# Seven products for eight in the second MoE matmul: Strassen's algorithm on pairs of token tiles, with its sums on VectorE

## The chip, the cores and the metric

One core of one Trainium2 chip runs the kernel. The metric is the device time of one execution in microseconds (us), given as the median of several executions. The profile is taken of one execution, so its span differs a little from the median. PE is TensorE, DVE is VectorE, ACT is ScalarE, POOL is GpSimd, SP is SyncE; a q behind the name (SPq, ACTq) is the engine's sequencer, which here issues DMAs.

## The reference, cut to what matters

```python
# q, k, v: (8 batches, 12 heads, 448 tokens, 64); w_in: 768 x 2048; w_out: 2048 x 768
scores = q @ k.T / sqrt(64)
attn   = softmax(scores) @ v              # (8, 12, 448, 64)
x      = attn, heads side by side          # 3584 tokens x 768
h      = x @ w_in                          # first MoE matmul, 3584 x 2048
g      = h * sigmoid(h)
out    = g @ w_out                         # second MoE matmul, 3584 x 768, fp32
```

## The kernel before

Everything runs in fp16 with fp32 sums in PSUM, and the kernel's buffers there limit how much work may be under way: four banks are shared by h, the attention output a, and the outputs of the second matmul; two tiles of two banks each take scores. A score matmul uses only 32 of the 128 rows of the array (one head's half), and the kernel issues four of them for four different strips of rows, which overlap in the trace. A *burst* is a set of scores between two other kinds of work. Each score tile holds two heads. A burst for one score tile is called "one-bank" here, a burst for both tiles "both-bank".

The second matmul gives one PSUM bank 16 products of 128 tokens by 384 outputs, one for each 128 of the 2048 inner elements; ScalarE copies the bank out and SyncE's queue stores it:

```python
def ffn2(u, t, half):                      # 28 token tiles x 2 halves
    o = ps.tile([128, 512], FP32, tag="m", bufs=4)
    for f in range(NFF):                   # 16
        nc.tensor.matmul(out=o[:, 0:OH],   # OH = 384
            lhsT=g_t[(u, f)][:, 128 * t : 128 * (t + 1)],
            rhs=w_out_t[:, f, n0:n1], start=(f == 0), stop=(f == NFF - 1))

def store(u, t, half):
    ost = sb.tile([128, OH], FP32, tag="ost", bufs=6)
    nc.scalar.copy(out=ost, in_=o_t[(u, t, half)][:, 0:OH])
    for w in range(4):
        ...
        last = (u, t, half) == (B // 2 - 1, NT - 1, 1)
        eng = nc.scalar if last and w % 2 else nc.sync      # two queues at the very end
        eng.dma_start(out=dst[col // 32], in_=ost[32 * w : 32 * (w + 1), :])
```

The order of the instructions is worked out while the kernel is built, by a list scheduler in the kernel's own file: it keeps a clock, an estimated duration for each operation, and a count of free buffers ("rings"), and puts on each engine what is ready first. The parts (`...` marks cuts):

```python
t = sb.tile([128, TPP, 2, 32], FP16, name=f"rk_{b}_{hg}", tag="rk", bufs=3)   # raw k
t = sb.tile([128, g1 - g0, 2, 32], FP16, name=f"rq_{n}", tag="rq", bufs=4)    # raw q
...
rk_ring, rq_ring, v_ring = Ring(3), Ring(4), Ring(2)     # the scheduler's view of them
...
# scores of units 0 to 2 go bank by bank, later ones in both-bank bursts
split = ((0,), (1,)) if ns[0] < 3 else ((0, 1),)
...
for i in range(NWARM):                                   # 13 matmuls of zeros at the start ("warming")
    nc.tensor.matmul(out=z, lhsT=zeros[:, 0:128], rhs=zeros, start=True, stop=True)
```

The softmax here doesn't subtract the row's maximum and nothing guards it: scores larger than these inputs give would overflow.

## Time and profile before

| | before |
|---|---|
| time, median (range) of 3 | 425.92 us (425.27 to 426.13) |
| span of the profiled execution | 423.6 us |
| TensorE busy | 414.5 us, 98% |
| VectorE / ScalarE busy | 193.8 us / 242.5 us |
| first h product / first output product | 25.64 us / 60.18 us after the start |
| last product to end of span | 4.01 us |

The prediction below shows the page's head, the cut by stages and the prices. Two views that it tells but does not show are needed. The first is the waits of TensorE (columns: who waited, for whom; us in total, times, longest):

```profile
PE s L295 <- ACT E L331: 2.9, 6, 1.0
PE h L414 <- DVE g L432: 0.5, 1, 0.5
```

So TensorE waits for the exponentials at the start, and hardly for anything else. The second is the end of the timeline (columns: start us, duration, engine, line, what, how many):

```profile
404.86 16.07 SPq L464 DMA_DIRECT2D out_dram<-ost  x25
...
419.64 0.48 ACT L457 COPY ost<-o 128x384 f32<-128x384 f32 x1 [2.12 <-PE o L445]
420.15 0.86 ACTq L464 DMA_DIRECT2D out_dram<-ost  x2
```

(The view merges rows of one kind: the 16.07 us hold pauses of the queue.) The last copy follows the last product at once, and the last four stores go out on two queues, which are done 1.4 us after the last product (at 419.56).

### The profile page before, as it was taken

How to read it: one execution, taken by the hardware profiler on the slowest of the kernel's cores; microseconds unless marked ns; L12 is line 12 of the kernel's file. 1: busy time of each engine (PE TensorE's matmuls, PEld its weight loads, DVE VectorE, ACT ScalarE, POOL GpSimd, SP SyncE). 2: the span in 40 equal slices, each digit the busy share in tenths (PEclk: the TensorE clock that was granted, in tenths of full speed). 3: DMA queues.
4: the chain of work that ended last, by engine and by line, in shares of the span. 5: the costliest groups of instructions: out<-in, count | busy, mean ns of one | idle time of the engine just before them, and what ended most of it. 6: DMA issues, size and time to landing. Idle time of an engine off the chain costs nothing.

```text
span 423.6 us, 9512 instructions
## 1 busy us (share of the span) xinstructions
PE 414.5 (98%) x3933; PEld 212.4 (50%) x3933; DVE 193.8 (46%) x404; ACT 242.5 (57%) x373; POOL 95.3 (22%) x175
## 2 busy tenths in 40 slices
PE   7899999999999999999999999999999999999996
PEld 3567755444544444444344545544445565565563
DVE  4568746667333585725577154512354204403400
ACT  4678975697465777667766753465773114414411
POOL 6775656630005406200440700000000000000000
PEclk9589999999999999999999999999999999999999
DMA  8999999890024906712390941012100220031033
GB/s 119 201 194 184 148 182 218 126 174 3 15 63 65 204 5 90 125 44 53 34 165 21 156 91 39 2 28 53 34 2 11 51 67 24 2 74 40 0 76 74
DMA packets 37979, 34.45 MB, mean 81 GB/s; under 512 B 11952, under 2 KB 36400, under 8 KB 37936
## 3 DMA queue, kind: packets, MB, share of 16 engines
q0 software_dynamic: 27184, 22.82, 36.7%
q1 hardware_dynamic: 10656, 10.93, 10.1%
q8 instruction: 31, 0.51, 0.5%
q10 hardware_dynamic: 96, 0.10, 0.1%
q14 instruction: 12, 0.10, 0.1%
HBM read 45.61 MB, written 11.01 MB: 134 GB/s over the span
## 4 chain that ended last, share of the span: by engine, by line
PE 93%; ACT 2%; DMA 1%; POOL 1%; DVE 0%; issue 0%; ACTq 0%; DVEq 0%
PE o L445 35%; PE h L414 33%; PE a L347 14%; PE s L295 10%; ACT E L331 2%; PE z L856 1%; DMA rk<-in_k_dram 1%; POOL V L235 1%; DVE KT L271 0%; POOL rq L222 0%; POOL rk L216 0%; DVE g L432 0%; ACT ost L457 0%; DVE zeros L199 0%; DVE ones L197 0%
## 5 line engine op out<-in xcount | busy, mean ns | idle before, releaser
L331 ACT ACTIVATE E<-s 128x896 f16<-128x896 f32 (+1 forms) x172 | 148.9, 914 | 24.2 <-PE s L295 22.9
L414 PE MATMUL h<-xT,w_in_t 128*128 128x448 f16 (+1 forms) x864 | 153.6, 332 | 0.5 <-DVE g L432 0.5
L445 PE MATMUL o<-w_out_t,g 128*128 128x384 f16 x896 | 152.5, 326 | 0.0
L432 DVE SCALAR_TENSOR_TENSOR g<-th,h 128x448 f16<-128x448 f16 (+1 forms) x144 | 79.8, 564 | 98.2 <-ACT th L425 96.3
L445 PEld LDWEIGHTS <-g 128*128 128x128 f16 x896 | 84.7, 98 | 65.1 <-issue 11.6
L414 PEld LDWEIGHTS <-w_in_t 128*128 128x128 f16 x864 | 80.8, 98 | 69.2 <-issue 13.6
L425 ACT ACTIVATE th<-h 128x448 f16<-128x448 f32 (+1 forms) x144 | 71.6, 505 | 53.2 <-PE h L414 52.1
L457 ACT COPY ost<-o 128x384 f32<-128x384 f32 x56 | 26.8, 479 | 99.5 <-PE o L445 92.3
L235 POOL DMA_DIRECT2D V<-in_v_dram x88 | 48.9, 572 | 134.8 <-PE a L347 113.1
L295 PE MATMUL s<-QT,KT 32*128 32x448 f16 (+4 forms) x864 | 54.1, 344 | 3.2 <-ACT E L331 2.9
L271 DVE STREAM_TRANSPOSE KT<-rk 128x256 f16<-128x256 f16 (+2 forms) x96 | 31.7, 380 | 46.0 <-PE s L295 26.4
L400 DVE SCALAR_TENSOR_TENSOR xT<-a,rdn 128x448 f16<-128x448 f32 (+1 forms) x54 | 29.0, 568 | 34.0 <-PE a L347 33.7
L347 PE MATMUL a<-E,V 128*32 128x448 f16 (+3 forms) x864 | 42.0, 346 | 0.2 <-issue 0.2
L295 PEld LDWEIGHTS <-KT 32*128 32x128 f16 (+2 forms) x864 | 16.6, 101 | 32.0 <-issue 30.6
L347 PEld LDWEIGHTS <-V 128*32 128x32 f16 (+2 forms) x864 | 19.0, 98 | 23.5 <-issue 16.3
L282 DVE STREAM_TRANSPOSE QT<-rq 128x896 f16<-128x896 f16 (+1 forms) x27 | 26.3, 976 | 0.9 <-DMA rq<-in_q_dram 0.9
L383 DVE STREAM_TRANSPOSE sT<-a 128x448 f32<-128x448 f32 (+1 forms) x27 | 14.8, 576 | 26.0 <-PE a L347 26.0
L347 PE MATMUL a<-E,ones 128*32 128x448 f16 (+4 forms) x432 | 21.8, 349 | 0.0
L222 POOL DMA_DIRECT2D rq<-in_q_dram x27 | 15.5, 574 | 4.2 <-DMA rk<-in_k_dram 1.2
L347 PEld LDWEIGHTS <-ones 128*32 128x32 f16 (+2 forms) x432 | 9.5, 99 | 12.7 <-issue 9.0
L392 DVE STREAM_TRANSPOSE rdn<-inv 128x448 f32<-128x448 f32 (+1 forms) x27 | 14.5, 563 | 0.1
L216 POOL DMA_DIRECT2D rk<-in_k_dram x24 | 13.9, 580 | 2.8 <-DMA w_out_t<-in_moe_w_out_dram 1.7
(12 smaller groups left out, 33.3 us busy)
## 6 DMA issues: line engine op xcount, KB each, us to landing
out_dram<-ost SPq DMA_DIRECT2D x222, 48.0 KB, 1.6
rk<-in_k_dram POOLq DMA_DIRECT2D x24, 224.0 KB, 5.5
rq<-in_q_dram POOLq DMA_DIRECT2D x21, 224.0 KB, 6.3
w_in_t<-in_moe_w_in_dram POOLq DMA_DIRECT2D x24, 128.0 KB, 5.1
w_out_t<-in_moe_w_out_dram POOLq DMA_DIRECT2D x8, 384.0 KB, 8.7
V<-in_v_dram POOLq DMA_DIRECT2D x43, 64.0 KB, 4.7
V<-in_v_dram POOLq DMA_DIRECT2D x40, 48.0 KB, 4.5
rq<-in_q_dram POOLq DMA_DIRECT2D x6, 112.0 KB, 5.8
```

Source lines behind the costliest of these rows:

```text
L235: nc.gpsimd.dma_start(out=VT[b][32 * x : 32 * (x + 1), hs, 0:count, :], in_=v[b, hs].rearrange("h (i g) d -> i h g d", g=TPP)[:, :, first ...
L271: nc.vector.transpose(out=kt[:, e].rearrange("p c x i -> p x c i")[:, x:y, 0:count], in_=t[:, first : first + count * (y - x), e, :].rearr ...
L282: nc.vector.transpose(out=qt.rearrange("p e g i -> p g e i"), in_=rawq[n])
L295: nc.tensor.matmul(out=pS[p0 : p0 + 32 * (x1 - x0), h % 2, at : at + nq], lhsT=KT[(b, hg)][32 * h : 32 * (h + 1), e, c, x0:x1, :], rhs=QT[ ...
L331: nc.scalar.activation(out=E[(n, w)][0:kr, 2 * y : 2 * y + 2, :], in_=pS_t[(n, w, y)][0:kr, :, 0:S], func=AF.Exp, scale=attn_scale,)
L347: nc.tensor.matmul(out=a[32 * h : 32 * (h + 1), 0:nq], lhsT=w, rhs=e[k0:k1, h, at : at + nq], start=start, stop=stop,)
L400: nc.vector.scalar_tensor_tensor(out=xT[(b, cc)][:, 32 * g0 : 32 * g1], in0=acc[(n, part)][:, 0:nq], scalar=0.5, in1=rdn_t[n].rearrange("p ...
L414: nc.tensor.matmul(out=h[:, 0 : t1 - t0], lhsT=w_in_t[:, cc, 128 * f : 128 * (f + 1)], rhs=xT[(b, cc)][:, t0:t1], start=(cc == 0), stop=(c ...
L425: nc.scalar.activation(out=th, in_=h_t[(b, f, t0)][:, 0 : t1 - t0], func=AF.Tanh)
L432: nc.vector.scalar_tensor_tensor(out=g_t[(u, f)][:, S * r + t0 : S * r + t1], in0=th_t[(b, f, t0)], scalar=1.0, in1=h_t[(b, f, t0)][:, 0 : ...
L445: nc.tensor.matmul(out=o[:, 0:OH], lhsT=g_t[(u, f)][:, 128 * t : 128 * (t + 1)], rhs=w_out_t[:, f, n0:n1], start=(f == 0), stop=(f == NFF ...
L457: nc.scalar.copy(out=ost, in_=o_t[(u, t, half)][:, 0:OH])
```

## The change

Its intent is to make TensorE, which sets the end, do less. Two token tiles A (rows) by two halves of the inner elements, times two halves of the inner elements by two halves of the outputs, is a 2 x 2 matrix product of blocks. Strassen's algorithm does it with 7 block products (8 matmuls each) for 8, and pays with sums of blocks before and after. Thirteen of the fourteen pairs of tiles take it; the first stays plain, as the weight sums are not ready. The core of the diff:

```diff
-    def ffn2(u, t, half): ...            # 16 matmuls into one bank
+    def combine_g(qd, m, f0, f1):        # sums of gate outputs, fp16, VectorE
+        x, y, op = {
+            5: (rows(a, 0), rows(a, 1), ALU.add),
+            2: (rows(b, 0), rows(b, 1), ALU.add),
+            1: (rows(a, 0), rows(b, 1), ALU.add),
+            6: (rows(b, 0), rows(a, 0), ALU.subtract),
+            7: (rows(a, 1), rows(b, 1), ALU.subtract),
+        }[m]
+        ...
+        nc.vector.tensor_tensor(out=dst[:, f0:f1], in0=x[:, f0:f1], in1=y[:, f0:f1], op=op)
+
+    BANK = {3: 3, 5: 3, 4: 4, 2: 4, 1: 1, 7: 1, 6: 6}    # 5, 2, 7 accumulate on 3, 4, 1
+    def product(qd, m): ...              # 8 matmuls, 384 columns each
+    def take_3(qd):   nc.scalar.copy(out=tmp(qd, "s"), in_=bank(qd, 3))
+    def take_4(qd):   add(tmp_t[(qd, "s")], bank(qd, 4), tmp_t[(qd, "s")])
+    ...                                  # six fp32 sums of 384 elements for each pair
+    def take_7(qd):
+        add(ost(qd, 0, 0), bank(qd, 1), tmp_t[(qd, "s")])
+        store(qd, 0, 0)
```

`combine_w` makes the five weight sums once, in the same way, in ten instructions. With the algorithm came a new frame around it: smaller buffers, to make room in SBUF, another pacing of the scores, and other rules for the start:

```diff
-    PACE = 2.6
+    PACE = 3
-        t = sb.tile([...], FP16, name=f"rk_{b}_{hg}", tag="rk", bufs=3)     # ring 3 -> 2 too
+        t = sb.tile([...], FP16, name=f"rk_{b}_{hg}", tag="rk", bufs=2)
-        t = sb.tile([...], FP16, name=f"rq_{n}", tag="rq", bufs=4)          # ring 4 -> 3 too
+        t = sb.tile([...], FP16, name=f"rq_{n}", tag="rq", bufs=3)
-            split = ((0,), (1,)) if ns[0] < 3 else ((0, 1),)
+            split = ((0,), (1,)) if ns[0] < 6 else ((0, 1),)
-    for i in range(NWARM): ...           # 13
+        if warm["on"] and od.free["PE"] <= od.now and wait > 0.3 and od.now > 1.0:
+            n = max(1, int((wait - 0.1) / mm(512)))      # comes to 20
+            od.on_pe(Op("PE", n * mm(512), lambda n=n: run_zeros(n)), "full")
-            eng = nc.scalar if last and w % 2 else nc.sync
+            nc.sync.dma_start(...)       # all stores on one queue
```

## The prediction

> **What bounds the kernel now.** I read first the page's table of busy time, its row of slices and its chain, to see which engine sets the end.
>
> ```profile
> span 423.6 us, 9512 instructions
> ...
> PE 414.5 (98%) x3933; PEld 212.4 (50%) x3933; DVE 193.8 (46%) x404; ACT 242.5 (57%) x373; POOL 95.3 (22%) x175
> ...
> PEclk9589999999999999999999999999999999999999
> ...
> PE 93%; ACT 2%; DMA 1%; POOL 1%; DVE 0%; issue 0%; ACTq 0%; DVEq 0%
> PE o L445 35%; PE h L414 33%; PE a L347 14%; PE s L295 10%; ACT E L331 2%; PE z L856 1%; DMA rk<-in_k_dram 1%; POOL V L235 1%; DVE KT L271 0%; POOL rq L222 0%; POOL rk L216 0%; DVE g L432 0%; ACT ost L457 0%; DVE zeros L199 0%; DVE ones L197 0%
> ```
>
> TensorE is on the chain for 93% of the span, and the largest item on it, 35%, is "o", the second MoE matmul, which is what the change cuts. A busy PE alone proves little, because matmul records overlap; the chain and the absence of waits prove more. The cut by stages then shows where TensorE is really full (columns: stretch; length; PE, PEld, DVE, ACT, POOL busy with counts; granted clock; DMA share; GB/s).
>
> ```profile
> 0.00:10.00 10.00, 7.49 (x45) 3.11 (x46) 4.15 (x13) 3.68 (x4) 7.12 (x16) 1.00 0.81 114
> 10.00:20.00 10.00, 8.59 (x128) 5.41 (x127) 5.99 (x16) 6.99 (x9) 7.45 (x14) 0.52 1.27 200
> 20.00:30.00 10.00, 9.68 (x184) 6.57 (x184) 5.23 (x16) 7.07 (x12) 6.91 (x14) 0.79 1.11 200
> 30.00:40.00 10.00, 9.69 (x200) 7.57 (x192) 7.98 (x23) 8.93 (x16) 6.91 (x12) 1.00 1.13 177
> 40.00:280.00 240.00, 239.51 (x2392) 115.57 (x2390) 131.66 (x272) 160.12 (x241) 66.91 (x122) 1.00 0.56 91
> 280.00:420.00 140.00, 139.56 (x1005) 74.13 (x1003) 38.84 (x67) 55.55 (x95) 0.00 (x0) 1.00 0.16 39
> ```
>
> From 40 us on TensorE stands still for about 1 us of 380, at full clock, with VectorE 55% busy up to 280 us and 28% after. So a TensorE microsecond removed there is worth a microsecond, until another engine cannot follow. The first 40 us are another regime: half clock between 10 and 24 us, ACT and DMA in the way.
>
> Last I took the price of one product, from the groups by form and from the chain in order of time.
>
> ```profile
> L445 PE MATMUL o<-w_out_t,g 128*128 128x384 f16 x896 | 152.5, 326 | 0.0
> L457 ACT COPY ost<-o 128x384 f32<-128x384 f32 x56 | 26.8, 479 | 99.5 <-PE o L445 92.3 <-issue 7.2
> ...
> 63.45 2.71 PE o L445 x16
> 66.67 2.71 PE o L445 x16
> ...
> 398.76 20.81 PE o L445 x128
> ```
>
> The last row is the clean price: 128 back-to-back products in 20.81 us, 0.1626 us each (384 columns). The two rows above show a product group that alternates with a score burst of 8 matmuls: the period is 66.67 - 63.45 = 3.22 us, of which 16 x 0.1626 = 2.60 is product and 0.37 the burst (8 matmuls of 448 columns, four at a time, at 448/384 of the column time: 2 x 0.187). The rest, 0.25, is two changes between the whole array and its row tiles: about 0.11 to 0.12 us each.
>
> [...]here the 13 warming matmuls took 5.73 us, 0.44 us each, twice the full-clock time of 512 columns (0.217 by the same scaling).
>
> **The change part by part.** There are 28 token tiles, 14 pairs. The first pair stays plain: 4 groups of 16. Thirteen pairs take 7 products of 8 matmuls.
>
> Removed from TensorE: 896 - (64 + 13 x 56 = 728) = 104 matmuls. At 0.1626 us: -16.9 us. All lie after 60 us, so on the path.
>
> Added to TensorE: from the built instruction order the array changes mode 222 times instead of 200; 22 x 0.11 = +2.4 us. The order also has 20 warming matmuls for 13, 19 of them before the first scores. In the kernel before, the 13 end at 6.96 us just as the first transposed q is ready (6.94), so they cost nothing; six more at 0.22 to 0.44 us put the first scores back by 1.3 to 2.6 us, less if the clock comes up earlier. I take +1.5.
>
> Recovered at the start: units 3 to 5 now issue their scores one bank at a time, so that ACT can run exp on one while TensorE fills the other. Before, ACT shows gaps of 1.56, 1.57, 0.59 and some 0.3 us there, about 4 in sum; the array is at half clock, so I credit half: -2.
>
> [...]ACT loses 13 of 56 copies, 13 x 0.479 = -6.2 us, and goes to 236. [...]a gate or a reading of PSUM that comes late holds one of the four PSUM banks that h, a and p share. [...]I take +2 for TensorE waits, where there was 1.
>
> Moved: products 5, 2 and 7 accumulate on the bank of 3, 4 and 1 after that was read, so TensorE now depends on a copy or a sum in the middle of a pair. In the built order another pair's product or an attention step nearly always stands between [...], so I count nothing extra. Buffers for k, q, their transposes, E and xT shrink by a tenth to a third, to make room. The loads are asked for at 0.56 of the DMA in the middle stage, so I expect no loss after 60 us.
>
> The end: before, 4.0 us pass from the last product (419.57) to the end. Now product 6's four stores occupy the one SP queue (0.42 us an issue by the trace's median) until about 1.1 us after the last product, [...]its four issues end at 2.8; before, the two queues were done 1.4 us after the last product. So +1.4.
>
> Sum: -16.9 + 2.4 + 1.5 - 2.0 + 2.0 + 1.4 = -11.6; with 425.9 that makes 414.3. The order was evidently tuned anew with it (pacing of scores, priorities, starts allowed before the last operand of a group is there), which on average recovers something, so I set 413.5.
>
> **The rivals.** (1) VectorE becomes the bound in places. For: [...]four shared banks, a fresh dependence of sums on the last gates. Against: [...]the first three or four products of a pair need no sum. If it holds in half of the stretches, 8 to 12 us of TensorE waits come back: 421 to 425, within 2%. (2) The shared banks or smaller buffers give waits of TensorE on ACT or DMA. For: bank 3 of a pair is held across two products and two readings. Against: the interleaving of pairs. It would show as 3 to 6 us: 417 to 419. [...](4) TensorE saved all and nothing is given back: 425.9 - 16.9 = 409; with a better start 406.
>
> **Range and chances.** The arithmetic of products is sure to a microsecond; the start is good for 3 us either way, VectorE for 0 to 10 on the slow side. So 407 to 420 should hold it 8 times in 10. Faster by over 2% means under 417.4: it is about 4 us above my point, with one-sided risk from VectorE, 0.79. Within 2%: 0.18. Slower by over 2% needs the waits to exceed the whole saving by 8 us: 0.03.
>
> **What would show it.** Right: 792 product matmuls with about 134 us busy; idle TensorE time from 40 us on under 4 us; [...]the chain still over 90% TensorE; full clock from 40 us. Wrong: [...]TensorE rows with idle time released by VectorE sums or gates; loads of k, q and v landing later than now; the first scores after 9 us, or half clock beyond 25 us.

Passages that no trace or run of this case supports are cut out of the prediction, and the cuts are marked: all but the last measurement of one paragraph, the price of the added work on VectorE (130 gate sums, 78 fp32 sums, 10 weight sums and 32 gates cut in two) with the totals made from it, one rival, a few clauses and two signs. The forecast's sum came to -11.6 us, and 0.8 us for tuning made 413.5 us.

## More of the kernel before

Runs fall into groups by the mean clock that TensorE was granted (0.970 to 0.972 or 0.979 to 0.980 in nine of ten runs of the changed kernel), which turns out to matter. The series ran on different chips of the same kind, on which the median of the kernel before was 425.3 to 426.0 us; small differences between series have to be read with that in mind.

## The result, and the profile after

The changed kernel took 420.37 us (418.59 to 420.78, 4 runs) against 426.02 us (425.27 to 426.27) of the kernel before in the same rounds: a ratio of 0.9862, interval 0.9831 to 0.9894, so within 2%. Ratios here are the mean time of one kernel's runs over that of the other's of the same rounds, so not quite the ratio of the medians. The predicted 413.5 us was 7 us too low and the range, 407 to 420, did not hold it.

The head of the page after, with the chain of what ended last:

```profile
span 419.0 us, 9580 instructions
PE 404.6 (97%) x3836; PEld 203.8 (49%) x3836; DVE 285.2 (68%) x654; ACT 233.4 (56%) x360; POOL 95.2 (23%) x175
PEclk9659999999999999999999999999999999999998
PE 90%; DVE 4%; DMA 3%; issue 1%; ACT 1%; POOL 1%; DVEq 0%; POOLq 0%
```

TensorE is still the bound: 90% of the chain, and VectorE has 32% of its time free. The durations of VectorE's instructions, added up from the traces, rose by 109.9 us (from 211.4 to 321.3); neighbours overlap in time, so the busy time rose by 91.4 only, to 285.2. But the row of clocks (in tenths, 40 slices) shows 6 and 5 where the kernel before has 5 and 8. The cut by stages says where:

```profile
0.00:10.00 10.00, 7.93 (x44) 3.22 (x45) 3.99 (x12) 3.01 (x4) 6.12 (x15) 1.00 0.70 101
10.00:20.00 10.00, 8.38 (x128) 5.16 (x131) 4.71 (x13) 6.77 (x9) 6.88 (x14) 0.63 1.17 166
20.00:30.00 10.00, 8.91 (x148) 5.65 (x146) 3.85 (x11) 6.19 (x7) 5.88 (x11) 0.50 1.07 185
30.00:40.00 10.00, 10.00 (x152) 6.78 (x144) 6.52 (x20) 7.19 (x12) 8.41 (x14) 0.84 1.10 184
40.00:280.00 240.00, 237.53 (x2331) 116.48 (x2330) 175.96 (x398) 152.33 (x236) 64.63 (x117) 1.00 0.57 92
280.00:420.00 140.00, 131.86 (x1053) 66.56 (x1050) 90.20 (x203) 57.88 (x95) 3.28 (x6) 0.98 0.19 43
```

Asked for as one window, 20 to 40 us holds 292 matmuls on TensorE where the kernel before has 372, and idling explains little of it (1.1 us, before 0.6): the clock is at 0.50 for the whole of the third stretch and back at full speed only at about 33 us (0.84 of the fourth stretch, so 3.2 us of it at half speed), against 24 us before. From 40 us on, TensorE is idle for 2.5 us up to 280 us.

Three marks split the difference of the two profiled spans, 423.6 - 419.0 = 4.6 us. The work before the first output product is nearly the same in both (192 matmuls of h and 336 of attention; 272 of scores for 264, and 20 warming ones for 13), so the mark can be compared:

| stretch | before | after | change | prediction's terms |
|---|---|---|---|---|
| start to first output product | 60.18 | 67.06 | +6.9 | +1.5 - 2.0 = -0.5 |
| first output product to last | 359.38 | 344.79 | -14.6 | -16.9 + 2.4 + 2.0 - 0.8 = -13.3 |
| last product to end | 4.01 | 7.15 | +3.1 | +1.4 |
| sum | 423.6 | 419.0 | -4.6 | -12.4 |

The middle did a little better than predicted. What is missing is 7.4 us at the start and 1.7 us at the end. (Counted in the traces, 9 of the 22 added changes of mode lie before the first output product, so some 1.0 of the +2.4 us belongs to the first row.)

Two details of the new frame show at the start. GpSimd's timeline, first before:

```profile
3.50 0.57 POOL L216 DMA_DIRECT2D rk<-in_k_dram  x1
4.02 0.58 POOL L222 DMA_DIRECT2D rq<-in_q_dram  x1
4.54 2.51 POOL L235 DMA_DIRECT2D V<-in_v_dram  x4
```

and after:

```profile
6.38 0.53 POOL L222 DMA_DIRECT2D rk<-in_k_dram  x1 [2.84 <-DVE KT L277]
6.90 0.55 POOL L228 DMA_DIRECT2D rq<-in_q_dram  x1
7.42 2.49 POOL L241 DMA_DIRECT2D V<-in_v_dram  x4
```

With two k buffers, the third k load has to wait until VectorE has transposed the first k (2.84 us of idle time, released by KT), and V, which GpSimd issues after it, comes 2.9 us later (7.42 for 4.54 us). The other detail is the score bursts. Before, in TensorE's timeline:

```profile
21.88 0.93 PE L295 MATMUL s<-QT,KT 32*128 32x224 f16 x16
```

and after, at the same half clock:

```profile
21.74 0.93 PE L301 MATMUL s<-QT,KT 32*128 32x224 f16 x8 [0.98 <-ACT E L337]
...
23.47 0.93 PE L301 MATMUL s<-QT,KT 32*128 32x224 f16 x8
```

A both-bank burst of 16 matmuls takes 0.93 us, and so does a one-bank burst of 8. With two heads in it, a one-bank burst fills two of the four strips of 32 rows, and here, where it stands alone among other work, it took as long half full as full. That is a cost of splitting the bursts which the prediction did not see.

### The profile page after: what moved, and what is told of

Its sections match the earlier page's. It is cut to its first block, busy times and chain, and to the rows that moved or that the text cites. A ratio compares the mean times of both kernels' runs of the same rounds, so it can differ in the third digit from the quotient of the medians.

```text
span 419.0 us, 9580 instructions
## 1 busy us (share of the span) xinstructions
PE 404.6 (97%) x3836; PEld 203.8 (49%) x3836; DVE 285.2 (68%) x654; ACT 233.4 (56%) x360; POOL 95.2 (23%) x175
## 3 DMA queue, kind: packets, MB, share of 16 engines
q1 hardware_dynamic: 10752, 11.02, 10.5%
## 4 chain that ended last, share of the span: by engine, by line
PE 90%; DVE 4%; DMA 3%; issue 1%; ACT 1%; POOL 1%; DVEq 0%; POOLq 0%
PE h L420 36%; PE p L511 27%; PE a L353 14%; PE s L301 11%; PE o L525 3%; DMA V<-in_v_dram 2%; DMA rk<-in_k_dram 1%; DVE sT L389 1%; DVE KT L277 1%; ACT E L337 1%; DVE rdn L398 1%; DVE QT L288 0%; DVE ost L562 0%; DVE S L501 0%; POOL V L241 0%
## 5 line engine op out<-in xcount | busy, mean ns | idle before, releaser
L420 PE MATMUL h<-xT,w_in_t 128*128 128x448 f16 (+1 forms) x864 | 157.4, 333 | 0.0
L467 DVE SCALAR_TENSOR_TENSOR G<-th,h 128x448 f16<-128x448 f16 (+2 forms) x144 | 74.9, 529 | 57.7 <-ACT th L431 54.7
L301 PE MATMUL s<-QT,KT 32*128 32x448 f16 (+4 forms) x864 | 57.0, 348 | 3.2 <-ACT E L337 3.0
L511 PEld LDWEIGHTS <-G 128*128 128x128 f16 x384 | 36.6, 98 | 29.3 <-issue 5.7
L511 PEld LDWEIGHTS <-S 128*128 128x128 f16 x312 | 29.3, 98 | 23.2 <-issue 4.3
L511 PE MATMUL p<-D,G 128*128 128x384 f16 x208 | 37.8, 327 | 0.0
L511 PE MATMUL p<-w_out_t,S 128*128 128x384 f16 x208 | 37.0, 327 | 0.2 <-DVE S L501 0.2
L511 PE MATMUL p<-w_out_t,G 128*128 128x384 f16 x176 | 31.7, 326 | 1.2 <-DVE m L562 1.2
L501 DVE TENSOR_TENSOR S<-G 128x512 f16<-128x512 f16 x70 | 25.7, 414 | 5.5 <-PE p L511 5.4
L572 ACT COPY ost<-p 128x384 f32<-128x384 f32 x13 | 6.2, 480 | 29.3 <-PE p L511 29.3
```

The lines of the kernel that those rows point to most:

```text
L301: nc.tensor.matmul(out=pS[p0 : p0 + 32 * (x1 - x0), h % 2, at : at + nq], lhsT=KT[(b, hg)][32 * h : 32 * (h + 1), e, c, x0:x1, :], rhs=QT[ ...
L420: nc.tensor.matmul(out=h[:, 0 : t1 - t0], lhsT=w_in_t[:, cc, 128 * f : 128 * (f + 1)], rhs=xT[(b, cc)][:, t0:t1], start=(cc == 0), stop=(c ...
L467: nc.vector.scalar_tensor_tensor(out=dst[:, f, at + lo : at + hi], in0=th_t[(b, f, t0)][:, lo - t0 : hi - t0], scalar=1.0, in1=h_t[(b, f, ...
L501: nc.vector.tensor_tensor(out=dst[:, f0:f1], in0=x[:, f0:f1], in1=y[:, f0:f1], op=op)
L511: nc.tensor.matmul(out=pr_t[(qd, BANK[m])][:, 0:OH], lhsT=w[:, f, :], rhs=W_[m][:, f, :], start=(f == 0 and BANK[m] == m), stop=(f == HF - 1),
```

## The experiments

Three theories for the lost 7.4 us of the start and one for the end. *Loads*: the smaller k and q buffers hold up V and w_in. *Bursts*: the one-bank bursts of units 3 to 5 cost more time than they let ScalarE gain. *Warming*: seven more warming matmuls delay the scores. *Stores*: the one store queue makes the end longer. Their common rival was the prediction's own first rival, VectorE, and the doubt whether the products were saved at all. Times are medians; "before" is the kernel before in the same rounds.

**1. The same frame with plain products.** All fourteen pairs as 16-matmul groups, no sums; all else as changed.

```diff
-                queue_quad(qd)
+                for t in (2 * qd, 2 * qd + 1):
+                    for j in range(2):
+                        queue_plain(t, j)
...                                  # no weight sums, dependences on plain groups
```

> The changed kernel with every pair of tiles done by 2 x 2 plain groups of 16 products; order rules, buffers, loads, warming matmuls and splits as in the changed kernel. No sums on VectorE. Theory (the products save what was counted, about 17 us less 5 for switches, VectorE waits and the later end; the start and the new frame lose about 6): 431 to 433 us, so slower than the kernel before. Rival (the products themselves save little because of waits on VectorE and banks): 422 to 425 us.

Measured: 433.22 us (431.57 to 434.01), ratio 1.0174 [1.0149, 1.0200] to before. So the frame alone is 7.7 us slower than the kernel before, and Strassen's products in that frame are worth 433.2 - 420.4 = 12.8 us. By the three marks of its profile: first output product at 66.44 us (+6.3 against before), from there to the last product 360.65 us (before 359.38, changed 344.79: the products and their waits save 15.9 us), and 4.42 us from the last product to the end. The late start belongs to the frame and not to the sums; the longer end belongs to Strassen's part, since the plain groups share the single store queue and end sooner.

**2. VectorE relieved.** The 130 gate sums left out and the products taken from unsummed gates: the result is wrong, the load of TensorE the same.

```diff
+        w[5], w[2], w[1] = rows(2 * qd, 0), rows(2 * qd + 1, 0), rows(2 * qd, 1)
...
-        nc.vector.tensor_tensor(out=dst[:, f0:f1], in0=x[:, f0:f1], in1=y[:, f0:f1], op=op)
```

> The changed kernel without the 130 gate sums on VectorE (products 5, 2 and 1 take a gate tile in place of the sum, so the result is wrong on purpose); planned order the same. VectorE loses some 54 us of busy time. Theory that VectorE waits are small (about 2 to 3 us of idle TensorE between 120 and 240 us): 417.5 to 419.5 us. Rival (VectorE is a hidden bound): 410 to 415 us.

Measured: 419.54 us (418.43 to 420.00), VectorE busy 243.7 us. Taking 42 us of work off VectorE moves the time by 0.8 us in the medians; at equal granted clock (see experiment 5) it is 0.3 us slower to 0.7 us faster, and the ratio to before, 0.9861, is that of the changed kernel. VectorE is not a hidden bound.

**3. Warming.** The fill of the start capped at 13 warming matmuls in total.

```diff
-            n = max(1, int((wait - 0.1) / mm(512)))
+            n = min(max(1, int((wait - 0.1) / mm(512))), 13 - warm.setdefault("n", 0))
...                                  # nothing issued once 13 are out
```

> The changed kernel with at most 13 warming matmuls in place of 20. First scores at about 6.95 us instead of 7.68. Theory that the extra ones only delay: 419.3 to 420 us. Rival (they keep the array's clock up): half clock from earlier or for longer, over 421 us.

Measured: 420.29 us (420.00 to 422.02). The first scores came at 6.99 instead of 7.68 us, but full clock came no earlier (23.9 us of half clock against 20.5, though its profile is of the slowest of its four runs), and the time is the same. The theory falls as a cause of the loss. The clock records of the traces show why nothing is won: with 13 warming matmuls the first stretch of full clock lasts only from 7.1 to 10.5 us, with 20 from 5.8 to 12.6 us. It is so in nearly all profiles: 6.83 us in all 13 with 19 or more warming matmuls, 3.41 us in five of the six with 13. So the extra ones do cost TensorE time, and seem to get it back in clock.

**4. A third k buffer, order remade.** Buffer and ring both set back to three; and the reverse in the kernel before.

```diff
-        ... tag="rk", bufs=2)
+        ... tag="rk", bufs=3)
-    rk_ring, rq_ring, v_ring = Ring(2), Ring(3), Ring(2)
+    rk_ring, rq_ring, v_ring = Ring(3), Ring(3), Ring(2)
```

> The changed kernel with three buffers for k as before, in place of two (nothing else edited; the order is made anew). Theory of the loads (the third k load, and behind it in GpSimd's queue v and w_in, waits for the first k transpose): v loads issued near 4.6 us instead of 7.4, no wait of attention on v, first h at 26 to 29 us instead of 31.3, 415 to 418 us. Rival (the order of scores and the half clock set the start, the loads are hidden): 419.5 to 421 us.

> The kernel before with two buffers for k in place of three. Theory of the loads: v loads near 7.4 us, w_in about 3 us later, first h and the first second-stage group 2 to 5 us later, 428 to 431 us. Rival (loads are hidden): 425.5 to 426.5 us.

Measured: 421.00 us (420.75 to 423.96) in the changed kernel, no gain. V was issued at 4.55 us, as the theory says, but the first output product came at 69.69 us with 27.3 us of half clock. The scheduler, seeing another ring, had made another order; and the profile is of the slowest of the four runs (clock 0.962, the others 0.970), so even the later start is not the order's for certain. The kernel before with two k buffers took 427.83 us (426.59 to 428.09), 2 us more than before; there, too, the order was remade (in its trace 1,428 of the 3,933 matmuls stand elsewhere). So neither run tells loads from order, and the edit was the wrong one: it moved two things.

**5. Wider buffers with the order held.** Only the physical buffers grow (k to 3, q to 4; one output stage fewer makes the room), the scheduler's rings stay. The order on every engine stays the same (the traces of these runs differ from that of the changed kernel no more than that of an unaltered control does).

```diff
-    NSG, NTMP, NOST = 3, 3, 6
+    NSG, NTMP, NOST = 3, 3, 5
-        ... tag="rk", bufs=2)
+        ... tag="rk", bufs=3)
-        ... tag="rq", bufs=3)
+        ... tag="rq", bufs=4)
```

> The changed kernel with three physical k buffers and four q buffers as in the kernel before (one output stage fewer pays for the space); the order of work on every engine stays exactly that of the changed kernel, which the earlier run with a third k buffer could not hold. Loads theory (about a third of the lost start is the smaller load buffers): V and w_in are issued about 2.9 us earlier, TensorE's 1.2 us wait for V at 15 to 16 us is gone, the first h comes 1 to 3 us earlier than 31.3 us, and the time is 417.5 to 419 us. Rival (the order of the bursts is the whole loss of the start, the loads only wait for it): V earlier, but first h within 0.5 us of 31.3 and the time 419.5 to 421 us.

Measured: 417.67 us (417.33 to 419.56), ratio 0.9820 [0.9795, 0.9846]. That looks like the loads theory exactly: V at 4.55 us, TensorE's 1.2 us wait for V gone, first h at 28.66 and first output product at 63.60 us. But the four runs were not alike: three had a mean granted clock of 0.979 or 0.980, one (the slowest) 0.972, where the changed kernel had one of 0.979 (the fastest, 418.59 us) and three of 0.971 or 0.972. So a control and two repeats went in the same rounds: the changed kernel unaltered, the same wide buffers, and the third k buffer alone.

> The changed kernel once more, unaltered, so that the wider buffers are compared on one chip, in the same rounds, with enough runs to sort them by granted clock. Four runs so far: three at a mean clock of 0.971 (420.1 to 420.8 us) and one at 0.979 (418.6 us). If that is chance, the same mix comes again: a median near 420 us, spread 418.5 to 421.

> Three k and four q buffers with the order held, again. Reading A (the buffers are worth 2.7 us[...]): median 417.3 to 418.3 us and most runs at 0.979. Reading B (they are worth about 1 us, and the rest of the 2.7 was the luck of four runs): median 419 to 419.6 us and the same mix of clocks as the control. In both, runs of equal clock differ by about 1 us.

> Only the third k buffer, order held. If k is what held up V and w_in (the third k load waited for the first k transpose), this gives all of what the run with both gives: within 0.4 us of it. If the q buffers carry it, within 0.4 us of the control.

Measured: control 419.67 us (417.67 to 421.04), wide buffers 419.25 us (417.49 to 419.61), k alone 417.43 us (417.30 to 418.02). Sorted by granted clock, with the runs of before:

| kernel | clock 0.979 or 0.980 | clock 0.970 to 0.972 |
|---|---|---|
| changed kernel (two series) | 418.1 us (3 runs) | 420.6 us (6 runs) |
| k and q wider (two series) | 417.5 us (4) | 419.4 us (4) |
| k wider | 417.5 us (4) | none |

(One run of the changed kernel, 419.26 us, lay between at 0.975.) At equal clock the buffers are worth 0.6 to 1.2 us (0.3 to 1.3 if only the last series is taken, whose runs shared chip and rounds), and the 2.7 us were for the most part the luck of four runs: reading B. Why the k buffer alone had the higher clock in four of four is not settled by four runs.

The control's own profile shows the other state of the same kernel. The page's stretches in the control:

```profile
10.00:20.00 10.00, 8.89 (x137) 5.39 (x136) 5.26 (x15) 7.22 (x10) 6.56 (x13) 0.65 1.15 154
20.00:30.00 10.00, 9.20 (x174) 6.03 (x173) 4.38 (x12) 6.95 (x9) 6.24 (x12) 0.67 1.03 170
30.00:40.00 10.00, 10.00 (x182) 7.13 (x171) 7.36 (x20) 8.25 (x15) 7.61 (x13) 1.00 1.09 191
```

and its first output product:

```profile
63.94 2.29 PE L525 MATMUL o<-w_out_t,G 128*128 128x384 f16 x13
```

Half clock ends at about 26.6 us here (0.67 of the stretch, so 6.6 us at half speed), not at 33; the whole stretch lasts 13.65 instead of 20.48 us, and the first output product comes 3.1 us earlier. (TensorE's wait for V, by the way, is absent from this profile too, without wider buffers.) Of the +6.9 us at the start, then, 3.8 are there also when the clock is kind, and 3.1 are one longer stretch of half clock, which 6 of 10 runs of the changed kernel had, by their mean clock. The kernel before is not split like this: its 39 runs have clocks from 0.978 to 0.984 and means of 425.5 us at either end.

The 3.8 us can be looked into, because this profile has as long a half clock (13.65 us) before the first output product as the kernel before, and as much idle time of TensorE (4.6 us in both). TensorE's busy time with scores up to that mark, first before, then in the control:

```profile
0.00:60.18 60.18, 17.57 (x264) 0.89 1.10 169
0.00:63.94 63.94, 20.29 (x272) 0.89 1.06 160
```

The same view gives 5.73 and 7.09 us for warming matmuls, 14.64 and 14.66 for attention, 20.63 and 20.83 for h. So 2.7 us more go to scores and 1.4 to warming; these counts overlap a little, and TensorE's busy time as a whole rose by 3.75 us (from 55.62 to 59.37). One burst of 8 matmuls, 0.4 us by the prediction's price, is among these scores, because it now stands before the mark and not after it; the other 2.3 us are what the same scores cost more in this order.

**6. The bursts.** First by the same way as in experiment 4: both-bank bursts for units 3 to 5 in the changed kernel, one-bank bursts for them in the kernel before.

```diff
-            split = ((0,), (1,)) if ns[0] < 6 else ((0, 1),)      # changed kernel
+            split = ((0,), (1,)) if ns[0] < 3 else ((0, 1),)
```

> The changed kernel with the scores of units 3 to 5 issued for both banks in one burst, as in the kernel before (a burst for one bank uses two of the four row strips, so it takes as long as one for both). Theory of the half-filled bursts (in the half-clock start each of 12 extra bursts costs TensorE about 0.93 us of which half could be hidden[...]): first h at 26 to 29 us, full clock by 28, 414 to 417 us. Rival (the start is set by loads or ACT, and the split was a help): 420 to 423 us.

> The kernel before with the scores of units 3 to 5 issued one bank at a time, as the changed kernel does. Theory of the half-filled bursts: first h at 29 to 32 us, half clock until after 30, 429 to 432 us. Rival (the split helps or is neutral): 424 to 426.5 us.

Measured: in the changed kernel 428.29 us (426.92 to 433.04), which is worse by 8. Its start was in fact much better, first output product at 61.98 us and only 10.2 us of half clock; but the remade order left holes later, 5.3 us of TensorE idle time between 120 and 240 us and a second period of half clock of 13.65 us there. In the kernel before, the one-bank bursts cost 5.1 us (430.77 against 425.70; ratio 1.0125 [1.0091, 1.0159]), with the first output product at 66.66 us, just where the changed kernel has it, and half clock for 23.9 us (in its profile, which is of the slowest of the four runs). The scheduler's order differs from that of the kernel before only in the first third and then comes back to it, so this is the cleanest of the burst runs: the cost lies at the start, with the bursts and what the scheduler does around them. The half clock is 10.24 us longer than before, worth up to 5.1 us by itself, so here much of the cost may come by way of the clock. To get a good order in the changed kernel too, the pace was set to 2.8, with a control that changes the pace alone:

```diff
-    PACE = 3
+    PACE = 2.8
```

> Control for the next run: the changed kernel with the pace of score bursts at 2.8 in place of 3 in the planner, nothing else. The order changes in small places only. Both theories: 419 to 422 us, first h near 31 us.

> The control (pace 2.8) with the scores of units 3 to 5 again for both banks in one burst. With pace 3 this edit won 5 us at the start and lost more between 80 and 240 us, where the planner left TensorE without MoE work; with 2.8 its plan has no such hole. Theory of the half-filled bursts: first h at 26 to 29 us, first second-stage group near 62 us instead of 67, and the 5 us are kept: 414 to 417 us, 4 to 6 under the control. Rival (the time won at the start always comes back as waits later): within 1.5 us of the control.

Measured: 419.44 us (418.84 to 420.27) for the control, so the pace alone does nothing that can be told; 416.59 us (416.25 to 417.69) with both-bank bursts, 2.85 us less (4 to 6 had been expected), ratios 0.9863 [0.9843, 0.9882] and 0.9799 [0.9779, 0.9819] to before. The first output product moved from 65.10 to 62.82 us, and the half clock from 13.65 to 10.24 us. The slowest of its runs is faster than the fastest of the control. The credit of 2 us that the prediction gave to the one-bank bursts is in truth a cost. TensorE's busy time with scores up to the mark fell from 20.06 to 17.60 us, about as much as the mark moved. How much of it is their own time and how much the clock that comes up later with them, these two runs do not separate: 3.41 us less of half clock is worth up to 1.7 us. The control of experiment 5, where the half clock is no longer than before and the scores still cost some 2.3 us more, shows that the clock is not all of it.

**7. Does a half-filled array keep the clock down?** A guess, which no run had shown: the clock is granted by how full the array is. Then a full-width matmul of zeros behind each one-bank burst should bring the clock up sooner.

```diff
+        if n >= 2 and len(ys) == 1 and not h_t:
+            run_zeros(1)
```

> The changed kernel with one full-array warming matmul behind each one-bank score burst from unit 2 on until the first h (15 or so more of them, about 0.43 us each at half clock). Theory that the half-filled array keeps the clock low: full clock comes back before 28 us instead of near 33, and the time stays within 2 us of the changed kernel because the fillers cost what the clock wins. Rival (clock set by something else): half clock to 33 us or later and 3 to 5 us slower.

Measured: 429.52 us (427.37 to 431.50), with half clock for 37.55 us in the profile, which is of the slowest run; the mean clock of the four, 0.951 to 0.964, is below that of every run of the changed kernel. The cut by stages of this run:

```profile
10.00:20.00 10.00, 8.93 (x119) 4.85 (x113) 4.47 (x12) 6.33 (x8) 7.36 (x15) 0.59 1.23 176
20.00:30.00 10.00, 10.00 (x101) 5.10 (x99) 3.37 (x9) 4.45 (x5) 6.85 (x13) 0.50 1.12 193
30.00:40.00 10.00, 10.00 (x108) 5.10 (x106) 1.90 (x6) 4.14 (x6) 5.69 (x9) 0.50 1.14 193
```

TensorE, as the trace models it, has no gap at all from 20 to 40 us, and the clock stays at one half. The theory falls: filling TensorE with zeros did not bring the clock back, and what brings it back is left open.

**8. The end.** Every other store of the last pair's last two output blocks goes to ScalarE's queue, much as the kernel before had it.

```diff
-            nc.sync.dma_start(
+            last = qd == NT * B // 4 - 1 and i == j and w % 2
+            (nc.scalar if last else nc.sync).dma_start(
```

> The changed kernel with two of the four stores of the last pair's blocks 00 and 11 issued from ACT, as the kernel before does for its last block. The trace shows the SP queue issuing without a break for the last 17.5 us, at about 0.46 us a store, until 4.5 us after the last product's sum. Theory that this queue sets the end: four issues fewer, 1.5 to 2 us saved, 418.4 to 419 us. Rival (the landing or something else sets the end): within 0.5 us of the changed kernel.

The order on TensorE is untouched. Measured: 417.75 us (416.96 to 418.47), and 5.78 us from the last product to the end instead of 7.15. At equal clock (two runs each) 417.0 against 418.1 and 418.5 against 420.6 us: 1.1 to 2.1 us, so the rest of the 2.6 between the medians is clock again. In the changed kernel SyncE's queue from 405 us on and the last sum read:

```profile
405.90 10.98 SPq L557 DMA_DIRECT2D out_dram<-ost  x24
...
411.89 0.56 DVE L562 TENSOR_TENSOR ost<-p,s 128x384 f32<-128x384 f32 x1 [0.27 <-PE p L511]
```

24 stores are issued without a break, one every 0.46 us, until 416.88 us. (The expectation above speaks of 17.5 us without a break: a view from 395 us on shows 32 stores as one row, but the queue pauses for 2.1 us before 405.90.) The last sum is done at 412.45 us, so 4.4 us of the end are the queue working off what it has, and 2.1 us the last landing. The prediction let the queue be free for the last four stores 1.1 us after the last product; the trace has the first of them start at 415.12 us, 3.3 us after it. Its 0.42 us is the duration of one issue, which holds; the spacing is 0.46.

**9. Together.** Pace 2.8, both-bank bursts, 13 warming matmuls and stores on two queues; then the same with the wider buffers.

> The changed kernel with pace 2.8, both banks in one burst for units 3 to 5, 13 warming matmuls, and the last stores on two queues. If the three effects add: control minus 5 (bursts), minus 0.5 (zeros), minus 2.5 (stores): 411 to 414 us. Rival (they overlap, or the order without the planner's fillers falls into half clock again): 416 to 419 us.

> The same wider buffers in the kernel with pace 2.8, bursts for both banks, 13 warming matmuls and the last stores on two queues (415.6 us), again with the order unchanged. Loads theory: 412.5 to 414 us, first h 1 to 2 us before 28.1. Rival: 415 to 416 us, first h at 28.

Measured: 415.59 us (414.71 to 416.83), ratio 0.9777 [0.9749, 0.9805], so the three effects do not add to the 411 to 414 us expected, and the start has 17.07 us of half clock; and 414.32 us (413.96 to 414.64), ratio 0.9730 [0.9713, 0.9746], faster than both kernels and the only run whose whole interval lies below 0.98. By clock, the wider buffers gain nothing here that can be told (414.71 against 414.6 us at 0.979). Its page begins:

```profile
span 412.9 us, 9571 instructions
PE 400.0 (97%) x3829; PEld 202.2 (49%) x3829; DVE 286.0 (69%) x654; ACT 232.5 (56%) x360; POOL 95.4 (23%) x175
```

By the three marks: first output product at 62.29 us, 344.81 us from there to the last product, 5.77 us to the end. The middle is the changed kernel's to a hundredth; all of the gain over it is at the two ends, 4.8 us and 1.4 us.

## Why the prediction was wrong, point by point

*The products held, and the mode switches as far as can be told.* Promised were -16.9 and +2.4 us. In the same frame, Strassen's products saved 15.9 us between the first output product and the last, where -16.9 and the +2.0 of waits make -14.9 (the plain frame has 224 changes of mode by the built order, the changed kernel 222, so switches do not enter here). Against the kernel before, the middle gained 14.6 us where the terms and the 0.8 for tuning say 13.3. The traces account for it: 13 of the 22 changes of mode lie there (13 x 0.11 = +1.4), TensorE idles 1.71 us instead of 0.49 (+1.2), and one burst of scores went ahead of the mark (-0.4); with -16.9 that makes -14.7. No experiment changed the switches alone. The plain frame fits their price: its middle has 15 more of them than the kernel before, the same moved burst, 0.2 us less idle time, and takes 1.28 us longer, which makes 0.12 us each. (The prediction's 0.187 us for 448 columns is 0.190 by its own scaling; its 0.11 to 0.12 stands.)

*VectorE held.* The kernel before has no such sums, so none had been measured when the prediction was made. Sorted by form, the three kinds of sums in the changed kernel (columns: form, count; busy us, mean ns; idle before, released by):

```profile
L501 DVE TENSOR_TENSOR S<-G 128x512 f16<-128x512 f16 x70 | 25.7, 414 | 5.5 <-PE p L511 5.4
L562 DVE TENSOR_TENSOR s<-p,s 128x384 f32<-128x384 f32 x13 | 7.2, 551 | 11.0 <-PE p L511 10.9
L457 DVE TENSOR_TENSOR D<-w_out_t 128x1536 f16<-128x1536 f16 x6 | 5.5, 929 | 0.0
```

So a gate sum of 512 fp16 elements took 414 ns, an fp32 sum of 384 elements with PSUM 551 and a weight sum of 1536 fp16 elements 929, and VectorE is at 68%. For the fp32 sums the kernel before could have given an estimate: its scalar_tensor_tensor takes 616 ns for 448 elements and 381 for 224, and a straight line through the two makes 549 for 384. In the changed kernel, with its 218 added sums and smaller buffers, the loads of k landed 4.3 us after their issue in the median and those of q 5.2 (before: 5.5 and 6.3), those of w_in 5.6 (before: 5.1). TensorE's waits on VectorE, as they read:

```profile
PE p L511 <- DVE m L562: 1.2, 1, 1.2
...
PE p L511 <- DVE xT L406: 0.3, 1, 0.3
PE p L511 <- DVE S L501: 0.2, 1, 0.2
```

1.7 us in all, where the kernel before has 0.5 of such waits after 40 us: +1.2, against the +2.0 that were set. The first rival, VectorE as the bound at 421 to 425 us, would have given nearly the measured time for a reason that experiment 2 excludes: a time that fits is no proof of its cause.

*The step that failed is the start*, "+1.5" for warming and "-2.0" recovered by the one-bank bursts, -0.5 in sum. Measured are +3.8 us in a run with the shorter stretch of half clock and +6.9 with the longer. Within it:

The credit for the bursts had the wrong sign. The idle time of ScalarE between 20 and 40 us was real, but the split did not fill it: ScalarE was busy for 16.0 us of these 20 before, for 13.4 in the changed kernel and 15.2 in the control. A split burst that stands alone costs TensorE twice (0.93 us for each half, at half clock): some 2.3 us of busy time with scores in the control, and the first output product comes 2.3 us later with it (experiment 6; 5 us of time in the kernel before). So -2.0 should have been about +2.3.

The half clock went the wrong way. The prediction had named "half clock beyond 25 us" as a sign of being wrong, and it lasted to 26.6 or 33 us; the longer one is the other 3.1 us.

The warming term was about right as TensorE time (1.4 us in the control), but taking the extra matmuls away gave nothing back (experiment 3), so it is no part of what can be recovered.

The smaller load buffers are worth 0.6 to 1.2 us of time, and 0.2 to 0.4 us by the first output product, in the start (experiment 5). The prediction expected no loss from buffers "after 60 us" and set nothing for the start, though "loads of k, q and v landing later than now" is among its signs of being wrong; V was issued 2.9 us later.

What makes the clock fall back and return stays open. The stretches of half clock at the start lasted 10.24, 13.65, 17.07, 20.48, 23.9, 27.3 or 37.55 us in the profiles, all near multiples of 3.41 us, and no run tells why. The step of 6.83 us is worth 0.6% in the changed kernel (420.6 against 418.1 us, experiment 5), as much as most effects. Open, too, are the other parts of the new frame: the smaller buffers for transposed k and q, exponentials and xT, and the scheduler's new priorities were not tested alone, and the best version still has its first output product 2.1 us later than the kernel before (62.29 against 60.18 us).

*The end was undersized*: +1.4 predicted, +3.1 measured. The mechanism was named (one queue, four last stores), but the queue's backlog was undersized: 24 issues in a row, which leave it free for the last four 3.3 us after the last product and not 1.1; two queues took back 1.4 us.

*The 0.8 us for "tuned anew"* was hope; the new frame as a whole costs 7.7 us (experiment 1). The middle needs no such term. And the chance of 0.79 for faster rested on a one-sided risk from VectorE; the start was taken as good for 3 us either way and missed by 4.3 in the kinder state, 7.4 in the profiled one. The second rival, "shared banks or smaller buffers" at 417 to 419, was right in naming the buffers and wrong in the size and the place: TensorE's one wait on a load is 1.2 us for V, at 15 us.

## What to carry to other kernels

When TensorE's work is cut in the steady part of a kernel, price the frame that comes with the cut too: the buffers given up, the order of the start, the last stores. Run the new frame with the old products once; here that one run told in one line that the saving was real (12.8 us) and the frame ate 7.7 of it. And before a difference of 2 us is believed, sort the runs by granted clock, and hold the order of the instructions fixed while a buffer is changed: an edit that lets a scheduler think anew measures the scheduler.
